# Issuing the second half of a weight matrix from ScalarE instead of SyncE at the start of an attention kernel

## Chip, cores and metric

The kernel runs on one core of a Trainium2 chip. The metric is device time in microseconds, in the median of several runs. Each run also has a *span*, from the first to the last traced instruction; for the kernel before it is about 1.7 us under the time.

## The reference, cut to what matters

```python
def _B_ref(x, wqkv, wo):              # x: 1 x 2048 x 1024, wqkv: 1024 x 3072
    qkv = (x @ wqkv) ...              # the kernel starts with the v columns, 2048..3071
    ... local dilated attention over 8 keys ...
x = A_x
g = _sigmoid((x * gate_w).sum(-1, keepdims=True))
return g * _A_ref(x, A_wqkv, A_wo) + (1 - g) * _B_ref(x, B_wqkv, B_wo)
```

Only the first stage matters: `v = x @ wqkv[:, 2048:3072]` of branch B. It is done in 16 token tiles of 128 rows times two halves of 512 columns. One (tile, half) takes eight matmuls, one per 128 rows of the weights.

## The kernel before

The kernel is a Python program that records operations with their dependencies. A list scheduler then orders them per engine from its own estimates of durations, and the emitted instruction order on every engine is fixed from then on.

```python
def load_x(t, prio):                   # token tile t, transposed on the way in
    return P.op("sp", lambda e: e.dma_start_transpose(xT[:, :, t*128:(t+1)*128], ...),
                1.5, writes=[...], prio=prio, chan="x%d" % t, lat=1.3)

def load_w(slot, half, src, c0, prio, d0=0, d1=8, eng="sp", after=()):
    n = d1 - d0
    return P.op(eng, lambda e: e.dma_start(ws[slot][:, d0:d1, half*512:half*512+512], ...),
                0.4 + 0.2 * n, writes=[...], prio=prio, ..., lat=0.55 * n, after=after)

load_x(0, 0)
load_w(0, 0, Bw, 2048, 0.1, 0, 2, "act")     # half 0, four quarters of 256 KB
load_w(0, 0, Bw, 2048, 0.2, 2, 4, "act")
load_w(0, 0, Bw, 2048, 0.3, 4, 6)
load_w(0, 0, Bw, 2048, 0.4, 6, 8)
for t in range(1, NT):
    load_x(t, 3 + t)
for d in range(0, 8, 2):                     # half 1, quarters 0 to 3
    load_w(0, 1, Bw, 2560, 6.1 + 0.1 * d, d, d + 2)
# ... cut ...
for t, half in [(4*b + i, half) for b in range(NT//4) for half in range(2) for i in range(4)]:
    # ... cut ...
    step = 2 if t == 0 else 8
    for d in range(0, 8, step):
        o = group(bank, xs, w, [xr, ws[0].part((d, d+step), ...)], d, d + step)
    move(vt[:, :, 0:32], ...)                # eviction, on ScalarE or VectorE
    P.op("sp", ...)                          # store v to HBM
```

By priority (lower goes first) SyncE issues transposes 1 to 3 (transpose t loads token tile t), then weight quarters 0 to 3 of half 1 (6.1 to 6.7), then transpose 4 (7) and so on. TensorE does tiles 0 to 3 of half 0, tiles 0 to 3 of half 1, then tiles 4 to 7 of half 0.

## Time and profile before

| | kernel before |
|---|---|
| time, median of 3 runs | 486.82 us (486.45 to 486.95) |
| span of the profiled run | 485.2 us |
| TensorE busy | 474.2 us, 98% |
| first matmul of the first stage | 5.54 us |
| TensorE without a pause from | 15.30 us |

The page of the kernel before, its busy table and its chain of work that ended last, cut to the lines used:

```profile
PE 474.2 (98%) x4339; PEld 222.8 (46%) x4403; DVE 285.2 (59%) x547; ACT 140.2 (29%) x227; POOL 5.9 (1%) x36
...
PE 95%; SPq 2%; issue 1%; DMA 1%; ACT 0%; DVE 0%
```

The kernel is bound by TensorE. SPq is SyncE's queue of DMA issues; it and DMA are the 3% of the chain that lie in the first 15 us. Here is that part of the chain in order of time (start us, us, what):

```profile
6.95 1.31 SPq L1308
8.26 0.04 issue
8.31 0.58 SPq L1313
...
9.44 0.47 SPq L1313
9.91 0.04 issue
9.96 5.07 DMA w<-in_B_wqkv_dram
15.02 0.27 issue
15.30 10.74 PE ps_all L1334 x49
```

L1308 is a transpose, L1313 a weight load; L1334 is the helper that emits all groups of matmuls (edits move it to L1332 or L1337 in other kernels, so go by the names: `w,xT` is this first stage). The chain reads: SyncE issues transpose 3, then the four quarters of half 1, the last of which takes 5.07 us to land; from 15.30 us on TensorE is its own bound. TensorE in the same stretch, as a timeline (start us, us, then the group and, in brackets, its idle time and what ended it):

```profile
5.54 1.47 PE L1334 MATMUL ps_all<-w,xT 128*128 128x512 bf16 x6 [0.28 <-DMA xT<-in_A_x_dram]
7.25 0.60 PE L1334 MATMUL ps_all<-w,xT 128*128 128x512 bf16 x2 [0.24 <-DMA w<-in_B_wqkv_dram]
8.17 6.82 PE L1334 MATMUL ps_all<-w,xT 128*128 128x512 bf16 x30 [0.32 <-DMA xT<-in_A_x_dram]
15.30 1.03 PE L1334 MATMUL ps_all<-w,xT 128*128 128x512 bf16 x4 [0.30 <-DMA w<-in_B_wqkv_dram]
```

A matmul is drawn as 379 ns long, but the next one starts 0.216 us after it, so the idle numbers in brackets are about 0.16 us too small. "Lost time" below is the distance between two starts less 0.216 us. In this trace it is 0.40 and 0.48 us before 8.2 us, and 0.16 and 0.47 us for quarters 2 and 3.

The DMA engines in two stretches (stretch, its length, busy time of each engine, clock, DMA share, GB/s):

```profile
7.50:14.50 7.00, 6.68 (x31) 2.75 (x30) 0.69 (x1) 1.80 (x3) 0.00 (x0) 1.00 1.14 255
9.50:10.50 1.00, 1.00 (x6) 0.47 (x5) 0.00 (x0) 0.39 (x1) 0.00 (x0) 1.00 0.56 110
```

The DMA share is the summed packet time over the time of 16 engines, and overlapping packets take it over 1. The engines are full, apart from one hole between transpose 3 and the first quarter.

### The profile page before, as it was taken

Reading aid. Unit: us, or ns where it says so; the run is one execution under the profiler, and the core shown is the slowest. Engines: PE = TensorE matmul, PEld = TensorE weight load, DVE = VectorE, ACT = ScalarE, POOL = GpSimd, SP = SyncE. Lnnn points to the kernel's source line nnn. Section 1 sums busy time; section 2 is a strip of 40 time slices with the busy share of each in tenths; the row PEclk is TensorE's granted clock in tenths of the full one; section 3 lists DMA queues with packets and bytes.
Section 4 is the critical chain, followed back from the end, with each engine's and each line's share of the span. In section 5 each row is a group of like instructions: output and inputs, shape, how many; then the busy total and the mean of one; then the engine's idle time right before and its main releaser. Section 6 shows DMA issues by size and latency. Waiting matters only on the chain.

```text
span 485.2 us, 10105 instructions
## 1 busy us (share of the span) xinstructions
PE 474.2 (98%) x4339; PEld 222.8 (46%) x4403; DVE 285.2 (59%) x547; ACT 140.2 (29%) x227; POOL 5.9 (1%) x36
## 2 busy tenths in 40 slices
PE   8999999999999999999999999999999999999997
PEld 3444444444444444454544554444444444444443
DVE  2121435888688888665666556496579236653434
ACT  2111121235322234334443333455532230111000
POOL 4000000000000000000000000000000000000000
PEclk9999999999999999999999999999999999999999
DMA  8999993132014459433222322820086018830212
GB/s 224 222 194 299 309 355 122 65 110 86 1 44 135 107 138 245 100 76 86 55 75 67 85 66 66 204 54 2 10 217 163 1 15 242 221 24 2 88 68 89
DMA packets 72951, 57.39 MB, mean 118 GB/s; under 512 B 37953, under 2 KB 60865, under 8 KB 72898
## 3 DMA queue, kind: packets, MB, share of 16 engines
q1 hardware_dynamic: 72210, 56.07, 44.3%
q8 instruction: 36, 0.59, 0.5%
q10 hardware_dynamic: 688, 0.59, 0.4%
q14 instruction: 17, 0.14, 0.1%
HBM read 34.49 MB, written 13.76 MB: 99 GB/s over the span
## 4 chain that ended last, share of the span: by engine, by line
PE 95%; SPq 2%; issue 1%; DMA 1%; ACT 0%; DVE 0%
PE ps_all L1334 78%; PE ps_all L1693 11%; PE ps_all L1463 2%; PE ps_all L1440 2%; SPq L1308 1%; DMA w<-in_B_wqkv_dram 1%; PE ps_all L1556 1%; SPq L1313 1%; PE ps_all L1638 0%; PE ps_all L1610 0%; ACT e L1341 0%; DVE o L1697 0%
## 5 line engine op out<-in xcount | busy, mean ns | idle before, releaser
L1334 PE MATMUL ps_all<-w,xT 128*128 128x512 bf16 x924 | 208.6, 379 | 4.5 <-issue 2.1
L1334 PE MATMUL ps_all<-xT,w 128*128 128x512 bf16 x745 | 166.3, 379 | 2.2 <-issue 1.4
L1334 PEld LDWEIGHTS ps_all<-w,xT 128*128 128x128 bf16 x960 | 91.2, 98 | 111.1 <-DMA w<-in_B_wqkv_dram 2.1
L1334 PEld LDWEIGHTS ps_all<-xT,w 128*128 128x128 bf16 x768 | 73.9, 98 | 88.7 <-issue 1.3
L1693 PE MATMUL ps_all<-w,qT 128*128 128x512 bf16 (+1 forms) x260 | 55.4, 372 | 0.2
L1693 PEld LDWEIGHTS ps_all<-w,qT 128*128 128x128 bf16 x264 | 25.9, 98 | 29.6
L1365 DVE CAST vst<-ps_all 128x512 bf16<-128x512 f32 x15 | 10.4, 694 | 43.5 <-PE ps_all L1334 43.5
L1448 ACT ACTIVATE E<-ps_all 128x1824 bf16<-128x1824 f32 (+1 forms) x18 | 30.4, 1689 | 13.4 <-PE ps_all L1440 13.4
L1345 DVE TENSOR_SCALAR e<-e 128x512 bf16<-128x512 bf16 x64 | 18.4, 290 | 26.9 <-ACT e L1343 14.0
L1697 DVE SCALAR_TENSOR_TENSOR o<-ps_all,gm,xT 128x512 bf16<-128x512 f32 (+1 forms) x25 | 18.0, 728 | 21.1 <-PE ps_all L1693 20.8
L1341 ACT ACTIVATE e<-ps_all 128x512 bf16<-128x512 f32 x32 | 19.1, 598 | 39.0 <-PE ps_all L1334 38.1
L1343 ACT ACTIVATE e<-ps_all 128x512 bf16<-128x512 f32 x32 | 19.1, 598 | 32.3 <-PE ps_all L1334 32.3
L1295 DVE TENSOR_TENSOR mx<-mx,kT 128x1024 bf16<-128x1024 bf16 x32 | 20.9, 688 | 10.9 <-ACT kT L1366 10.8
L1295 DVE TENSOR_TENSOR mx<-mx,qT 128x1024 bf16<-128x1024 bf16 x32 | 20.8, 687 | 7.9 <-ACT qT L1369 7.9
L1451 DVE TENSOR_TENSOR E<-E,msk 128x1824 bf16<-128x1824 bf16 (+1 forms) x18 | 19.9, 1104 | 7.8 <-ACT E L1448 7.4
L1366 ACT ACTIVATE vst<-ps_all 128x512 bf16<-128x512 f32 x17 | 10.2, 601 | 48.5 <-PE ps_all L1334 45.1
L1480 DVE TENSOR_TENSOR ot<-ps_all,rs 128x512 bf16<-128x512 f32 x36 | 23.3, 686 | 0.0
L1366 ACT ACTIVATE az<-ps_all 128x512 bf16<-128x512 f32 x22 | 13.2, 601 | 34.5 <-PE ps_all L1334 34.5
L1366 ACT ACTIVATE kT<-ps_all 128x512 bf16<-128x512 f32 x20 | 11.9, 597 | 37.6 <-PE ps_all L1334 37.6
L1347 DVE SCALAR_TENSOR_TENSOR pk<-ps_all,e 128x512 bf16<-128x512 f32 x32 | 22.0, 689 | 0.7
L1369 ACT ACTIVATE qT<-ps_all 128x512 bf16<-128x512 f32 x19 | 11.4, 598 | 37.4 <-PE ps_all L1334 37.3
L1369 ACT ACTIVATE xT<-ps_all,g 128x512 bf16<-128x512 f32 x10 | 6.9, 689 | 45.1 <-PE ps_all L1334 45.1
(72 smaller groups left out, 260.2 us busy)
## 6 DMA issues: line engine op xcount, KB each, us to landing
rb<-rc_hbm SPq DMA_DIRECT2D x32, 256.0 KB, 5.2
w<-in_A_wqkv_dram SPq DMA_DIRECT2D x6, 1024.0 KB, 9.0
v<-vB_hbm SPq DMA_DIRECT2D x36, 132.0 KB, 2.7
vB_hbm<-vst SPq DMA_DIRECT2D x32, 132.0 KB, 6.2
w<-in_B_wqkv_dram SPq DMA_DIRECT2D x4, 1024.0 KB, 9.5
xn<-in_A_x_dram SPq DMA_DIRECT2D x16, 256.0 KB, 2.7
out_dram<-o SPq DMA_DIRECT2D x15, 256.0 KB, 2.1
oB_hbm<-ot SPq DMA_DIRECT2D x36, 96.0 KB, 2.2
```

The source lines that it names most:

```text
L1295: P.op("dve", lambda e, m=m, op=op: e.tensor_tensor(m[:, 0:n], m[:, 0:n], src, op), 0.08 + n / 1920.0, reads=[m.all(), reg], writes=[m.all()],
L1334: last = e.matmul(bank.ap(), lhs(dc), rhs(dc), start=(dc == 0), stop=(dc == 7))
L1341: P.op("act", lambda e: e.activation(e_[:, :], bank.ap(), ACT.Exp), act(512), reads=[bank.iv], writes=[e_.all()])
L1343: P.op("act", lambda e: e.activation(e_[:, :], bank.ap(), ACT.Exp, accum_out=qe[:, col:col + 1]), act(512) + 0.1, reads=[bank.iv], writes= ...
L1345: P.op("dve", lambda e: e.tensor_scalar(e_[:, :], e_[:, :], 1.0, 1e-6, op0=ALU.min, op1=ALU.add), 0.25, reads=[e_.all()], writes=[e_.all()])
L1347: P.op("dve", lambda e: e.scalar_tensor_tensor(out=dst, in0=bank.ap(), scalar=0.0, in1=e_[:, :], op0=ALU.max, op1=ALU.add), dps(512), read ...
L1366: fa = lambda e: e.activation(dst, src(), ACT.Copy)
L1369: fa = lambda e: e.activation(dst, src(), ACT.Copy, scale=scale)
L1448: P.op("act", lambda e: e.activation(E[:, 0:32 * nq].rearrange("p (j q) -> p j q", j=4), ps[:, 4:8, 0:8 * nq], ACT.Exp), act(32 * nq), rea ...
L1451: P.op("dve", lambda e: e.tensor_tensor(ev(), ev(), m[:, :, :].rearrange("p r q -> p (r q)")[:, None, :].to_broadcast([128, 16, 2 * nq]), ...
L1480: P.op("dve", lambda e, r=r, bv=bv, h=h: e.tensor_tensor(o[:, 512 * h:512 * h + 512].rearrange("p (k i c) -> p k i c", k=2, c=32), bv()[:, ...
L1693: last = e.matmul(bank.ap(0, f1 - f0), qT[:, dc, t * 128:(t + 1) * 128], ws[3][:, dc, f0:f1], start=(dc == 0), stop=(dc == 7))
```

## The change

The intent is to take the four quarter loads of half 1 from SyncE's queue, where they wait behind transpose 3, and let ScalarE issue them as soon as the second matmul group of tile 0 is done. SyncE then goes on with transposes 4, 5 and so on without a break.

```diff
         for t in range(1, NT):
             load_x(t, 3 + t)
-        for d in range(0, 8, 2):
-            load_w(0, 1, Bw, 2560, 6.1 + 0.1 * d, d, d + 2)
@@
                 o = group(bank, xs, w, [xr, ws[0].part((d, d + step), (half * 512, half * 512 + 512))], d, d + step)
+                if (t, half, d) == (0, 0, 2):
+                    for q in range(0, 8, 2):
+                        load_w(0, 1, Bw, 2560, 6.1 + 0.1 * q, q, q + 2, "act", after=[o])
```

## The prediction

> **What bounds the kernel.** TensorE: 474.2 of 485.2 us busy (busy table), 95% of the chain of waits, clock 1.00. In steady state a 512-column matmul starts every 0.216 us. After 15.3 us the waits view shows some 4 us of TensorE idle, none of it on a load, so the change can act only before 15.3 us.
>
> **What it could win.** From the matmul starts, idle between the first real matmul (5.54) and 15.3 us: 0.40 us for the last quarter of weight half 0 (landed 7.21), 0.48 for token tile 1 (8.13), then in the second half's first group 0.16 for quarter 2 (14.34) and 0.47 for quarter 3 (15.02). Only the last two, 0.63 us or 0.13% of the span, belong to the loads that move. The chain names them: SyncE's issues to 10.4 us, then a 5.07 us load.
>
> **What changes.** No work is removed. Four 256 KB loads (0.47 us of issue each) move from SyncE at 8.31–10.43 us to ScalarE's queue, after the second matmul group, which ends about 6.6. So they issue at 6.6–8.5 us, 1.7 us earlier. ScalarE has room (29% busy); its first eviction, at 7.90 us, slips to 8.5 or goes to VectorE, while seven banks wait. SyncE goes from transpose 3 (6.95–8.26) straight to transposes 4 and 5, needed only near 20.9 and 22.6 us.
>
> **What it costs.** The DMA engines are already full: share 1.05 at 8.0–9.5 us, 1.01 at 10.5–13.0 (windows); only 9.5–10.5 us is slack (0.56). That hole of 0.4–0.5 us is all that an earlier issue fills. The Trainium skill, "DMA: Bandwidth & Descriptors", section "Issuing engines are not separate DMA queues", says that queues of different engines run on the same 16 DMA engines and interleave, saving only issue time. This trace agrees: at 3.5–4.5 us ScalarE's queue moves 243 packets and SyncE's 378, taking 71% and 44% of the engines' time. So from about 7.8 us the weight quarters slow transposes 2 and 3, which one queue had served first, and transposes 4 and 5 then slow the weights.
>
> Estimate from packet times (46 ns per 1 KB weight packet, 18 ns per 256 B transpose packet; 1024 packets per transpose, 256 per quarter): a quarter is 0.74 us of all engines. Tile 2 landed at 9.14, needed at 9.91; behind one quarter it lands near 9.8. Tile 3 landed at 10.20, needed at 11.64; behind two quarters it lands at 11.7–12.3: a new wait of 0.1–0.6 us. Transposes 2–4 and the weights all fit by about 13.7 us, so the last quarter lands at 13.3–14.3, before its use at 14.7 plus the new wait: the 0.63 us disappears.
>
> Net −0.63 + (0.1 to 0.6), about −0.2 us. If weights take 71% of the engines, tile 3 lands near 13 and the kernel loses up to 1 us. The scheduler also redeals evictions between ScalarE and VectorE throughout; I allow ±0.5 us.
>
> **Predicted time** 486.6 us, 80% range 485.7 to 487.8. Faster by over 2%: 0.5%; within 2%: 99%; slower: 0.5%.
>
> **What would show it.** Right: four weight issues on ScalarE from 6.5–7 us; quarters landed by 14.3; no TensorE wait on weights after 13 us; tile 3 landing 1–2 us later than 10.20, with a wait before its group at 11.6; everything later shifted by one constant under 1 us. Wrong: tiles 2 and 3 landing as before (0.63 us won), or weights landing after 15 us.
>
> **What would make it wrong.** Transposes and copies on two queues stalling one another (transpose packets of up to 1.5 us are seen near 13.5 us), ScalarE's issue blocked, or a changed order of the later program opening new gaps.

## The result, and the profile after

| | before | change |
|---|---|---|
| time, median of 6 runs | 486.84 us (486.42 to 487.34) | 489.57 us (488.69 to 491.75) |
| ratio | | 1.0063, 95% interval 1.0042 to 1.0084 |
| profiled span, clock share | 485.2 us, 1.0 | 488.7 us, 0.996 |
| spans of the other runs of the change | | 486.9, 490.0, 487.6, 487.9, 487.8 us |

The kernel became 0.6% slower: the same by a 2% rule, but outside the predicted range of 485.7 to 487.8. The six runs also spread over 3 us, where those of the kernel before spread over 0.9.

The busy table and chain on the page of the change:

```profile
PE 476.8 (98%) x4339; PEld 223.9 (46%) x4403; DVE 287.2 (59%) x550; ACT 137.7 (28%) x224; POOL 5.9 (1%) x36
...
PE 95%; DMA 2%; SPq 1%; issue 1%; ACT 0%; DVE 0%
```

Its chain in the first 30 us:

```profile
6.97 1.31 SPq L1308
8.28 0.04 issue
8.32 7.76 DMA xT<-in_A_x_dram
16.08 0.14 issue
16.22 1.02 PE ps_all L1332 x4
...
17.29 12.43 PE ps_all L1332 x49
29.72 0.05 issue
```

The weights have gone from the chain. In their place stands transpose 4, issued at 8.32 us and 7.76 us on its way. And the next 49 matmuls took 12.43 us, where 49 took 10.74 us before. TensorE's timeline and the stretches of the change show both:

```profile
5.92 8.15 PE L1332 MATMUL ps_all<-w,xT 128*128 128x512 bf16 x34
16.22 5.95 PE L1332 MATMUL ps_all<-w,xT 128*128 128x512 bf16 x18 [2.14 <-DMA xT<-in_A_x_dram]
```

```profile
7.50:14.50 7.00, 6.57 (x31) 2.66 (x29) 1.39 (x2) 1.20 (x2) 0.00 (x0) 1.00 1.13 232
9.50:10.50 1.00, 1.00 (x7) 0.45 (x5) 0.00 (x0) 0.30 (x1) 0.00 (x0) 1.00 0.99 223
13.92:16.22 2.30, 0.16 (x2) 0.03 (x1) 0.00 (x0) 0.36 (x1) 0.00 (x0) 1.00 1.27 196
17.43:20.84 3.41, 3.41 (x9) 1.18 (x8) 0.00 (x0) 0.00 (x0) 0.00 (x0) 0.50 0.89 212
```

The hole at 9.5 to 10.5 us was filled (223 GB/s after 110), yet the DMA engines moved no more from 7.5 to 14.5 us (232 GB/s after 255). Counted by size in the packed traces, these 7 us held 1019 of the 1024 weight packets of half 1 and 2386 transpose packets in the kernel before, and 827 and 3035 in the change: transposes came in place of weights. TensorE did 34 matmuls, stood for 2.3 us, and from 17.43 to 20.84 us ran at a granted clock of 0.50.

34 matmuls are tiles 0 to 3 of half 0 and *one* quarter group of half 1. What TensorE waited for next was tile 4. The built program says why. This is TensorE's instruction order in the two programs, as (tile, half), q for a quarter group of tile 0:

```
before: (0,0) (1,0) (2,0) (3,0) (0,1)q0 q1 q2 q3 (1,1) (2,1) (3,1) (4,0) (5,0) (6,0) (7,0) ...
change: (0,0) (1,0) (2,0) (3,0) (0,1)q0 (4,0) q1 (5,0) q2 q3 (1,1) (2,1) (3,1) (6,0) (7,0) ...
```

The scheduler plans one DMA queue for all engines and 0.8 us for each ScalarE issue, so in its plan transpose 4 is issued (by 9.10 us) before quarter 1 (9.38). When quarter 0's group ends, tile 4 counts as there and quarter 1 as not. The scheduler moved tile 4 ahead of quarter 1, and tile 5 ahead of quarter 2.

The whole loss lies before the second stage. The time from the first matmul of the next stage to the end is 423.04 us before and 422.89 us in the change. The start of the next stage moved from 62.13 to 65.82 us, which is 0.15 us more than the spans differ.

A ledger of the two profiled runs. At their start, 0.38 us of later first matmul and three matmuls at half speed were nearly all absorbed by waits that the kernel before had there; 0.1 us stayed.

| | us |
|---|---|
| late start, what is left of it | +0.1 |
| wait for tile 4 (lost time at 13.91 us) | +2.31 |
| half clock: 3.41 us at 0.50, half of it lost | +1.7 |
| wait for quarters 2 and 3, gone | −0.63 |
| sum | +3.5 |
| span, 488.7 − 485.2 | +3.5 |

Two causes offered themselves. **Theory O**: the new TensorE order is what costs, since tile 4 is asked for 7 us before it used to be. **Theory C**, which a later call names **theory S** in a sharper form: the two DMA queues share the engines, so that weights and transposes delay one another whatever TensorE's order is. (It covers both the second queue and SyncE's earlier transposes 4 to 6.) A third question was the half clock (**theory W**: the wait brings it).

### The profile page after: what moved, and what is told of

Read it like the earlier page. It is cut to its first block, busy times and chain, and to the rows that moved or that the text cites. A ratio compares the mean times of both kernels' runs of the same rounds, so it can differ in the third digit from the quotient of the medians. Undisturbed runs are those within 1.5% of the kernel's fastest.

```text
span 488.7 us, 10100 instructions
## 1 busy us (share of the span) xinstructions
PE 476.8 (98%) x4339; PEld 223.9 (46%) x4403; DVE 287.2 (59%) x550; ACT 137.7 (28%) x224; POOL 5.9 (1%) x36
## 3 DMA queue, kind: packets, MB, share of 16 engines
q10 hardware_dynamic: 1776, 1.64, 1.4%
## 4 chain that ended last, share of the span: by engine, by line
PE 95%; DMA 2%; SPq 1%; issue 1%; ACT 0%; DVE 0%
PE ps_all L1332 78%; PE ps_all L1694 11%; PE ps_all L1464 2%; PE ps_all L1441 2%; DMA xT<-in_A_x_dram 2%; SPq L1308 1%; PE ps_all L1557 1%; PE ps_all L1639 0%; PE ps_all L1611 0%; SPq L1313 0%; ACT e L1339 0%; DVE o L1698 0%
## 5 line engine op out<-in xcount | busy, mean ns | idle before, releaser
L1431 DVE TENSOR_SCALAR qd<-qT,par 128x912 bf16<-128x912 bf16 (+1 forms) x34 | 14.6, 452 | 9.5 <-PE ps_all L1441 9.5
```

## The experiments

Landing times below are read from the DMA issues of each trace, one trace per kernel. "Next stage" is the start of the first matmul of the second stage.

| kernel | tile 3 | tile 4 | quarters 0, 1, 2, 3 | next stage | time, median |
|---|---|---|---|---|---|
| before | 10.20 | 16.56 | 11.54, 12.58, 14.34, 15.02 | 62.13 | 486.84 |
| change | 11.70 | 16.08 | 11.51, 12.84, 15.87, 16.96 | 65.82 | 489.57 |
| e1_order_kept | 11.60 | 16.13 | 11.11, 12.48, 15.08, 16.02 | 63.13 | 488.55 |
| e2_x4_held | 13.64 | 18.44 | 10.42, 13.44, 14.17, 14.71 | 63.77 | 488.13 |
| e3_order_alone | 10.24 | 16.06 | 12.53, 13.24, 13.98, 14.62 | 65.79 | 489.06 |
| e4_filler | 13.04 | 14.57 | 10.26, 11.28, 12.79, 13.84 | 65.11 | 491.00 |
| e5_one_ahead | 11.27 | 16.02 | 10.25, 13.13, 13.82, 14.54 | 61.73 | 486.70 |
| e6_two_ahead | 12.51 | 15.37 | 10.24, 11.47, 13.28, 14.01 | 61.78 | 486.92 |
| e7_in_turn | 10.32 | 19.59 | 13.20, 13.89, 15.13, 15.78 | 62.89 | 488.17 |
| e8_change_again | 13.79 | 15.45 | 10.20, 11.07, 13.55, 14.68 | 63.92 | 488.87, one run |
| e9_change_third | 10.19 | 14.48 | 12.14, 14.26, 15.65, 17.93 | 64.03 | 488.68, one run |
| e10_before_again | 10.93 | 17.04 | 12.57, 13.22, 14.36, 15.54 | 62.65 | 487.39, one run |

From the next stage to the end all twelve traces take 422.9 to 423.3 us, so every difference between the traces is made in the first stage. All kernels gave correct results. The kernel before had a median of 486.81 us (11 runs, spans 484.8 to 485.7, median 485.1) beside e1 to e4, 486.84 us (9 runs) beside e5 to e7, and 486.54 us (one run) beside e8 to e10.

### e1_order_kept: the change with TensorE's old order

```diff
+                if (t, half, d) == (0, 1, 6):
+                    first_half1 = o
+                if t >= 4 and half == 0:
+                    o.deps.add(first_half1)
```

> The change with one thing taken back: TensorE finishes token tile 0's second-half group before it goes to token tile 4, as in the kernel before; loads are issued as in the change. Theory O (the scheduler's new TensorE order, which puts tile 4's group in front of the weight quarters 1 to 3, is what costs): no wait on tile 4, no TensorE wait over 0.3 us after 13 us, time 486.2 to 486.9. Theory C (the two DMA queues slow one another, so the quarters land at about 16 and 17 us whatever TensorE's order is): TensorE waits on quarters 2 and 3 in tile 4's place, about 1.5 to 1.7 us more than before, time 488.2 to 489.2, in some runs more with a halved clock.

Measured: 488.55 us (487.93 to 489.62), ratio 1.0035 (1.0023 to 1.0047); spans 485.8 to 487.5, median 486.45, so 1.35 us over the kernel before. The clock share was 1.0 in all six runs. TensorE's timeline:

```profile
5.92 8.49 PE L1332 MATMUL ps_all<-w,xT 128*128 128x512 bf16 x36
15.13 0.60 PE L1332 MATMUL ps_all<-w,xT 128*128 128x512 bf16 x2 [0.72 <-DMA w<-in_B_wqkv_dram]
16.07 6.22 PE L1332 MATMUL ps_all<-w,xT 128*128 128x512 bf16 x28 [0.33 <-DMA w<-in_B_wqkv_dram]
```

With the order kept TensorE waits for quarter 2 and quarter 3 in tile 4's place. Theory O alone is out; C held in kind, with quarter 3 one microsecond earlier than it said (16.02). The quarters are issued earlier than in the kernel before (7.19 to 9.71 against 8.31 to 10.43 us) and the last of them lands *later*: by 1.0 us than in the first trace of the kernel before, by 0.5 us than in the second (e10). The DMA engines' stretch of e1:

```profile
7.50:14.50 7.00, 6.78 (x31) 2.56 (x29) 1.39 (x2) 1.20 (x2) 0.00 (x0) 1.00 1.08 253
```

They moved 253 GB/s, against 255 before. The transfer as a whole was not slowed down here; part of the same rate was spent on transposes 4 to 6, which TensorE did not need yet.

### e2_x4_held: e1, and transpose 4 waits for the weights

```diff
+                if t == 4:
+                    for q in range(0, 8, 2):
+                        e.wait_ge(P.csem["w0_1_%d" % q], 16)
                 return e.dma_start_transpose(...)
```

> As e1_order_kept, and SyncE waits before transpose 4 until the four weight quarters have landed, so that no later transpose shares the DMA engines with them; every other order is that of e1_order_kept. Theory O: same time as e1_order_kept within 0.2 us. Theory C: last quarter lands by 13.5 us instead of about 17, no TensorE wait on weights over 0.1 us, time 486.0 to 486.6, about 2 us under e1_order_kept. If the quarters still land at 15 us or later, C is wrong about transposes 4 to 6.

Measured: 488.13 us (487.36 to 489.12), ratio 1.0019 (1.0007 to 1.0032); median span 486.0, so 0.9 us over the kernel before. This missed what C said, and O's number too (0.42 us under e1, where O allowed 0.2). The quarters did land earlier (14.71 instead of 16.02), but now tile 3, in flight with them, landed at 13.64, and TensorE waited there:

```profile
13.69 8.59 PE L1337 MATMUL ps_all<-w,xT 128*128 128x512 bf16 x39 [1.66 <-DMA xT<-in_A_x_dram]
```

So the later transposes are at most one part of it. A tile that was issued *at the same moment* as the quarters pays as well. My expectation had taken tile 3's delay from the trace of the change (11.70), as if it were fixed.

### e3_order_alone: the kernel before with TensorE's order of the change

```diff
+                if (t, half) == (0, 1):
+                    late = [o] if d == 0 else late + [o]
+                if half == 1 and 1 <= t <= 3:
+                    o.deps.add(late[3])
+                if (t, half) in ((4, 0), (5, 0)):
+                    late[t - 3].deps.add(o)
```

> The kernel before, SyncE issuing all loads in the old order, with TensorE's order of the change forced on it. Theory O, as the only cause, says the order makes the loss: TensorE waits from about 13.8 us for tile 4, which landed at 16.56 us in the kernel before, so about 2.6 us of wait less the 0.63 us that it hides: 488.5 to 489.2, and in some runs 1.7 us more if the clock halves. If C is the only cause, tile 4 lands in time and the time stays within 0.4 us of 486.8.

Measured: 489.06 us (488.50 to 491.67), ratio 1.005 (1.0031 to 1.0069); median span 487.3, so 2.2 us over the kernel before. This is what O said, and C as the only cause is out: the order by itself, with all loads on one queue, costs nearly as much as the change. In the profiled run the wait was 2.46 us of lost time, and then the clock halved:

```profile
13.74:16.20 2.46, 0.16 (x2) 0.04 (x2) 0.00 (x0) 0.36 (x1) 0.00 (x0) 1.00 1.24 252
16.52:19.93 3.41, 3.41 (x10) 1.18 (x8) 0.00 (x0) 0.41 (x1) 0.00 (x0) 0.50 0.77 193
```

With e1 this makes a square of four, in median spans: neither 485.1, the new loads alone (ScalarE's earlier weights and SyncE's earlier transposes) 486.45, order alone 487.3, both 487.85 us. The two costs do not add up (+1.35 and +2.2 give +2.75). In the first trace of the change the waits overlap: while TensorE stands for tile 4 and then computes it, the late quarters land (15.87 and 16.96 us).

### e4_filler: idle matmuls in the change's wait

```diff
+                if (t, half, d) == (0, 1, 0):
+                    fill_after = o
+                if (t, half) == (4, 0):
+                    for i in range(9):
+                        f = P.op("pe", ...matmul of the warm-up tile into the spare bank..., after=[fill_after])
+                        o.deps.add(f)
```

> The change as it is, with nine idle matmuls on the spare PSUM bank placed in TensorE's order just before tile 4's group, where it waits 2.3 us. They take about 1.94 us at full clock. Theory W (the wait lets the clock halve in some runs, and that makes the spread and up to 1.7 us of the loss): no halved clock after the first 8 us in any run, times within 488.2 to 489.0, spread under 1 us. Rival (the halved clock has another cause): spread and median as the change, 488.7 to 491.8, median about 489.5, and clock shares under 0.998 in some runs.

Measured: 491.00 us (489.77 to 492.33), ratio 1.0088. The clock part held: no half clock after 4.76 us in the trace, and shares of 0.999 to 1.0 in all six runs, where two of the six runs of the change and two of e3 were at 0.996 or 0.997. That is weak evidence, since four halved runs in twelve can by chance be none in six. The time did not hold: the median is 2 us over W's range, and the spread 2.6 us. In the profiled run the delay had gone to tile 3:

```profile
13.09 4.06 PE L1332 MATMUL ps_all<-w,xT 128*128 128x512 bf16 x18 [0.62 <-DMA xT<-in_A_x_dram]
16.98 2.10 PE L1388 MATMUL ps_all<-warm 128*128 128x512 bf16 x9
18.93 3.40 PE L1332 MATMUL ps_all<-w,xT 128*128 128x512 bf16 x15
```

Tile 4 had landed at 14.57 us, so the nine fillers at 16.98 us covered no wait and were 1.94 us of plain cost. Why the other five runs were up to 2.6 us slower still is open; they have no trace. The run is consistent with theory W, but it does not test it in the trace, where no wait for tile 4 was left to fill, and it does not price the clock: that price comes from the trace of the change alone.

### e5_one_ahead and e6_two_ahead: earlier weights on the one queue

These leave all loads on SyncE and move quarter 0, or quarters 0 and 1, ahead of transpose 3. Tiles 4 and up stay behind tile 0's second half, as in e1.

```diff
-            load_w(0, 1, Bw, 2560, 6.1 + 0.1 * d, d, d + 2)
+            load_w(0, 1, Bw, 2560, 6.1 + 0.1 * d if d else 5.5, d, d + 2)          # e5
+            load_w(0, 1, Bw, 2560, 6.1 + 0.1 * d if d > 2 else 5.5 + 0.1 * d, d, d + 2)   # e6
```

> The kernel before, all loads on SyncE's one queue, with only weight quarter 0 moved up, between transposes 2 and 3 (so it fills the idle DMA time near 9.5 to 10.5 us), and tile 0's second-half group kept ahead of tile 4's. Theory S (the loss of the change is the sharing of the DMA engines between two queues, which lets late transposes and weights take turns, and not that the weights come earlier): quarter 3 lands by 14.2 us, tile 3 by 11.2 us, no TensorE wait over 0.2 us after 8.5 us, time 486.0 to 486.6, under the kernel before. Rival E (weights ahead of a transpose cost more than they win, whatever the queue): tile 3 lands after 12 us and TensorE waits for it, time 487.2 or more.

> As e5_one_ahead with quarters 0 and 1 ahead of transpose 3. Theory S: in order, tile 3 lands about 0.7 us later than in e5_one_ahead, near 11.6 to 12.0 us; TensorE has two quarter groups to do before it, so no wait over 0.2 us; time 486.0 to 486.7. Rival E: as e5_one_ahead or worse, 487.4 or more.

Measured: e5 486.70 us (486.61 to 487.20), ratio 0.9999 (0.9985 to 1.0013); e6 486.92 us (486.19 to 487.51), ratio 1.0003 (0.9989 to 1.0017). TensorE's timeline of e5 has no wait after 8.2 us:

```profile
5.92 2.01 PE L1334 MATMUL ps_all<-w,xT 128*128 128x512 bf16 x8
8.19 13.99 PE L1334 MATMUL ps_all<-w,xT 128*128 128x512 bf16 x63 [0.27 <-DMA xT<-in_A_x_dram]
```

The scheduler also put the moved quarters' groups before tile 3, which suits the new arrival order. So one or two quarters can come earlier than in the kernel before without any loss, if they come *in order* on one queue: landing times of tile 3 were 11.27 and 12.51 us, in the order of issue, and TensorE lost under 0.1 us for it. Theory S's numbers were narrowly missed (quarter 3 at 14.54 where it said 14.2, tile 3 of e6 at 12.51 where it said 12.0, times 0.1 and 0.2 us over its ranges), those of E by more (times of 487.2 and 487.4 or more). For one or two quarters E is out; four quarters ahead of transpose 3 on one queue were not tried.

The clearest pair is e2 and e5, one trace each. Both issue quarter 0 just before transpose 3 and the other quarters after it, and transpose 4 after them all. With two queues (e2) transpose 3 took 6.46 us from issue to landing, with one queue (e5) 3.68. And quarter 3, which e2 issued 1.4 us earlier (8.59 against 10.01 us), landed no earlier (14.71 against 14.54). The median spans are 486.0 and 485.0 us. So here the second queue costs something without the new order and without earlier transposes 4 to 6.

In the traces of e5 and e6 the next stage starts 0.4 to 0.9 us earlier than in the two traces of the kernel before, but the times differ by less than their spread. These are not a better kernel that I could show, only an equal one.

### e7_in_turn: ScalarE issues, but nothing shares

```diff
+                if eng == "act" and half == 1 and d0 == 0:
+                    e.wait_ge(P.csem["x3"], 16)
                 return e.dma_start(...)                 # on top of e2
```

> As e2_x4_held (ScalarE issues the weights, transpose 4 waits for them, TensorE's old order), and ScalarE waits for tile 3 to land before it issues the first quarter, so that no transpose and weight load are in flight together. Theory S: tile 3 lands near 10.2 us as in the kernel before; quarters 0 to 3 are issued at 10.3 to 12.2 us and land at 13.0 to 15.2; span within 0.4 us of 485.2 (the time may stay 0.3 us more, as the two kernels e1 and e2 showed between span and time). Theory Q (issuing from ScalarE's queue is itself slow): quarters land 1 us or more later than that, span over 486.2 us.

Measured: 488.17 us (487.48 to 488.30), ratio 1.0022 (1.0009 to 1.0036); median span 486.1, so 1.0 us over the kernel before. Tile 3 landed at 10.32 us, undelayed, as S said. Each quarter took 2.8 to 3.9 us from issue to landing, with no transpose beside it, against 3.2 to 5.1 in the kernel before, so ScalarE's queue is not slow by itself, and Q has no support. But quarter 3 landed at 15.78, later than the 15.2 that I allowed, since the first issue waited for tile 3 until 10.40 us and left the engines nearly idle meanwhile:

```profile
9.50:10.50 1.00, 1.00 (x6) 0.47 (x5) 0.00 (x0) 0.00 (x0) 0.00 (x0) 1.00 0.22 46
```

TensorE lost 1.16 us for quarters 2 and 3, where it lost 0.63 in the kernel before. The span misses S's number (485.6 at most) and stays just under Q's (over 486.2); the landing times are what decides between them.

### e8_change_again, e9_change_third, e10_before_again: second traces

No edit. One run and one trace each.

> The change once more, unaltered, for a second trace of it, since one trace cannot show whether its 2.3 us wait for tile 4 and its halved clock come in every run. If the wait on tile 4 is fixed by the order: tile 4 lands at 15 to 16.5 us again and TensorE waits 1 to 2.5 us for it. If the shared engines hand the delay to another tile: tile 3 lands at 12.5 us or later, TensorE waits there, and tile 4's wait is under 1 us. The halved clock after 13 us comes only if one idle stretch is over 2 us or so.

> As e8_change_again, a third trace of the change. Waits on tiles 3 and 4 and on the quarters together: 1.7 to 3 us in each trace, whichever tile bears them.

> The kernel before once more, unaltered, for a second trace. If its 0.63 us wait on quarters 2 and 3 is typical, quarter 3 lands at 15 us again. If not, it lands by 14.7 us as in e3_order_alone, which issues the loads in the same way, and the wait is under 0.3 us.

TensorE's timeline of e8:

```profile
13.84 8.37 PE L1332 MATMUL ps_all<-w,xT 128*128 128x512 bf16 x37 [1.48 <-DMA xT<-in_A_x_dram]
```

And of e9:

```profile
14.61 2.32 PE L1332 MATMUL ps_all<-w,xT 128*128 128x512 bf16 x9 [0.53 <-DMA xT<-in_A_x_dram]
18.28 4.04 PE L1332 MATMUL ps_all<-w,xT 128*128 128x512 bf16 x18 [1.34 <-DMA xT<-in_A_x_dram]
```

In e8 the wait is for tile 3 (1.64 us of lost time, after 0.13 for tile 2), and none is left for tile 4. In e9 it is for tile 4 (0.69) and then for tile 5 (1.51), which landed only at 18.14 us. In the first trace it was tile 4 alone (2.31). The same program thus loses 1.8 to 2.3 us, but which tile bears it changes from run to run. In e8 tile 4 (15.45 us) was in time, so there the wait is the sharing's and not the order's. Neither e8 nor e9 has a half clock after 8 us, and both spans (487.1 and 486.9 us) are 1.6 to 1.8 us under that of the first trace (488.7).

Which tile pays goes with a fraction of a microsecond in the moment of issue. Six traces have ScalarE's weights beside transpose 3. Where quarter 0 was issued before that transpose (e2, e4, e8; by 0.04 to 0.70 us), the transpose took 5.6 to 6.5 us to land; where 0.2 and 0.6 us after it (e1 and the first trace of the change), 4.6 and 4.7; where 0.95 us after it (e9), 3.5, as in the kernel before. The moment in turn follows TensorE, whose second group releases ScalarE: in the three traces of the change the clock was full from 7.19, 3.91 and 7.25 us, and quarter 0 was issued at 7.61, 6.88 and 7.64.

In e10 quarter 3 landed at 15.54 us and TensorE lost 0.64 us for it, so the wait that the change aimed at is a real one in the kernel before:

```profile
15.81 6.42 PE L1334 MATMUL ps_all<-w,xT 128*128 128x512 bf16 x29 [0.47 <-DMA w<-in_B_wqkv_dram]
```

## Why the prediction was wrong

The prediction said 486.6 us (485.7 to 487.8); the chip said 489.57 us. Two steps failed. The larger is the path: transposes 4 and 5 "needed only near 20.9 and 22.6 us". In the profiled run TensorE asked for tile 4 at 13.9 us and waited 2.31 us for it, and the new order alone (e3) costs 2.2 us of median span. The other is the overlap: "transposes 2–4 and the weights all fit by about 13.7 us". The last quarter landed at 14.68 to 17.93 us.

- **What bounds the kernel, and that only the first 15 us could change: right.** From the next stage to the end, all traces agree within 0.4 us.
- **The prize of 0.63 us: right in size, won by luck.** The wait was 0.64 us in the second trace of the kernel before, so the prize was there. It is gone in the first trace of the change, but not because the weights landed earlier, as predicted: they landed later (16.96 us), while TensorE was held up by tile 4. With the old order (e1) the same two quarters cost 1.38 us. Even e5, which waits for no weights, made the time no measurably shorter.
- **The weights issue at 6.6 us: about right, but late.** They were issued at 7.61, 6.88 and 7.64 us, since tile 0 landed when it would and the first matmuls ran at half clock in two of three traces.
- **"Tile 3 ... lands at 11.7–12.3: a new wait of 0.1–0.6 us": not a fixed size.** It landed at 11.70, 13.79 and 10.19 us, and cost nothing, 1.64 us and nothing. I had sized it as two quarters standing in front. With two queues the number of quarters that go first is not fixed. The second trace is nearer to the prediction's other branch ("tile 3 lands near 13").
- **"Transposes 2–4 and the weights all fit by about 13.7 us, so the last quarter lands at 13.3–14.3": this step failed.** It landed at 16.96, 14.68 and 17.93 us. The engines had few gaps (share 1.13 from 7.5 to 14.5 us), but I had added up packets at their median of 46 ns, and left out transposes 5 and 6, which SyncE now also issued. In those 7 us a weight packet took 76 ns in the mean (64 and 86 in e8 and e9), where it took 54 in the kernel before. From 7.5 to 14.5 us the engines moved 232, 261 and 210 GB/s in the three traces of the change, and 255 and 254 in the two of the kernel before: the rate did not rise on average, and part of it went to tiles that the old order did not need until 20 us. e1, which has these loads and the old order, costs 1.35 us of span.
- **"Needed only near 20.9 and 22.6 us": this step failed, and cost most.** "Everything later shifted by one constant" held from the second stage on, not before. I had named "a changed order of the later program" as a risk, but as a detail of evictions. It was the order of TensorE's first groups that changed, and e3 shows that this alone costs 2.2 us of median span. My estimate of when things are *needed* was taken from the old order, and the change moved the need itself to 13.9 us. The other risk that I had named, transposes and copies that stall one another on two queues, shows in the packet times above.
- **The half clock was not in the sum at all.** In the first trace it added 1.7 us after the 2.3 us wait. It goes with the slower runs: the two runs of the change with a clock share of 0.996 and 0.997 have spans of 488.7 and 490.0 us, the other four (0.999 and 1.000) have 486.9 to 487.9. Only the first of the two has a trace.

The sum, corrected in spans: +2.75 us for order and sharing together (square of four, which includes the half clock where it came), with the 0.63 us of the old wait already taken off.

Three things stay open. One is how the engines share out between two queues (the moment of issue goes with it, but six traces do not make a rule), and whether sharing also lowers the total rate, as the 210 GB/s of e9 would suggest and the 253 of e1 would not. Another is the rest of e4's slower runs. The third is that e1, e2 and e7 show a time 2.1 us over their span, where all others show about 1.7; that 0.4 us lies outside the trace.

## What to carry to other kernels

In these traces, loads on one queue landed in the order of issue (the kernel before, e3, e5, e6), and loads on two queues did not. Moving an urgent load to a second queue also let the less urgent ones behind it start at once and take their share. An earlier place in the same queue did no harm here (e5, e6), though it won nothing measurable either. With a kernel that a list scheduler orders, build the changed program's instruction order and read it before costing the change, because a moved load can move the consumer, and "needed at" times of the old profile no longer hold. And price the half clock that may follow a new TensorE wait; here it followed those of 2.31 and 2.46 us.

## What the Trainium skill lacked or had wrong

- "TensorE: Matmul & The Clock Gate", section "Why this matters for your kernels", says that gaps over about 3 us between bursts of matmuls bring the clock back to half. Here waits of 2.31 and 2.46 us were followed by a half clock (change and e3). It began about 1.2 and 0.3 us after the matmuls had resumed. Waits of 1.64 and 1.82 us (e8, e2) were not followed by one. The same page's section "What's actually happening" gives a free-running window of 3413 ns, and there the traces agree: each half-clock stretch lasted 3.41 us. Each also began three times 3.41 us after the moment from which the trace's clock record shows full speed (7.19 us to 17.43 in the change, 6.28 to 16.52 in e3), so the half clock came at the end of a stretch of 3.41 us in which TensorE had stood for 2.2 and 2.46 us. These are two cases, not a threshold.
- "DMA: Bandwidth & Descriptors", section "Issuing engines are not separate DMA queues", says that queues interleave on the same engines and a second one saves only issue time. The traces agree that both share the same engines: a second queue added no rate (253 GB/s in e1, 255 with one queue). The page lacks the cost: transpose 3, issued at about 7 us, landed 3.2 and 3.5 us later in the two traces of the kernel before, where the weights queue behind it, and 4.7, 6.4 and 3.5 us later in the three traces of the change, beside ScalarE's weights.
- The same page's section "Queues, rings and completion order" describes round robin by packet between queues. No page says how uneven it can be: in three traces of one program the last quarter landed at 14.68, 16.96 and 17.93 us.
